# Strassen's scheme for one more state projection, a chunked state tile and more sums by DMA, in a kernel bound by TensorE

## The chip, the cores and the metric

One core of a Trainium2 chip. The metric is device time in microseconds of the whole launch; the profile's span is some 1.8 us shorter than that time, as it runs from the first to the last instruction. The engines are called as the profile has them: PE (TensorE), PEld (its weight loads), DVE (VectorE), ACT (ScalarE), POOL (GpSimd), SP (SyncE).

## The reference

A layer norm feeds two branches: a diagonal complex state-space layer (2048 steps, 512 states) and a gated feed-forward layer (512 to 1792 to 512). Both are added to the input. Cut to what matters:

```python
xn = layernorm(x)                                   # x: 1 x 2048 x 512
Bu = einsum("bld,pd->blp", xn, B_bar)               # state projection (complex)
h  = Lam_bar * h + Bu[:, t]                         # a scan over 2048 steps
y  = 2 * einsum("blp,dp->bld", h, C).real + xn * Dskip
ff = (silu(xn @ w1) * (xn @ w3)) @ w2               # gate, up, down
return x + y + ff
```

## The kernel before

The 2048 tokens go through in four blocks of 512 (blocks 0 to 3). For each block PE computes 14 tiles of gate and up (`glu`), and the state projection `u`. PE writes its results to PSUM tiles; DVE or ACT must take them out before PE can use the tile again. DVE rotates `u` (the `pre` steps), scans it, rotates it back (the `post` steps) and so fills the state slots of the tile `act`, beside the gated products. Then PE multiplies `act` by one joint matrix of `w2` and `C`, in pairs of 128 tokens (pairs 0 to 7, `y_fast`), by Strassen's scheme: seven products for eight, at the price of sums of `act`: s1, s2 and s3 below, and s4 = a12 + s2, made after product 2 of the pair. A filler hands DVE its tasks in an order that it works out from a small model of the two engines. The order is then fixed: each engine runs its own list in order and waits on semaphores.

```python
def post_c(tsl=slice(0, TBLK)):              # last step that fills the states
    a, p16 = act_state(b, hf)[:, :, :, tsl], st["p16"][:, :, :, tsl]
    if (b, hf) == (NBLK - 1, 1):
        nc.vector.tensor_tensor(out=a, in0=a, in1=p16, op=ALU.add)
    else:
        gp.dma_start(out=a, in_=p16, accum_op=ALU.add)     # POOL queue, adds while it moves
...
def row_sums(n, b, p):                       # s3 = a11 - a21, s2 = s3 - a22, s1 = a21 + a22
    ...                                      # a22 holds the second half's states
    return [three, two, one] if n > 5 else [three, one, two]
...
def glu_last(b):                             # block 3: direct tiles first, then groups of four
    ...                                      # up tiles by Strassen: 7 products for 8
    for n in range(NG):
        product(g, a11, b11, True)           # g, e, f, z: four PSUM tiles, used again by each group
        copy(f, g)
        product(e, s1n, t1, True)
        ...
        add(lower[1][:, :, TH:TBLK], g)      # DVE: these adds free g and e for the next group
        product(e, s4n, b22, False)
        add(upper[1][:, :, TH:TBLK], e)
...
last_posts = ssm_tasks(3, middle=[(0.0, after_y2, None), *row_sums(4, *pairs[4])])
```

## Time and profile before

| | |
|---|---|
| time, median of 4 runs | 201.88 us (201.84 to 202.13) |
| span of the profiled run | 200.1 us |
| PE / DVE / ACT busy | 98% / 91% / 67% |
| first tile of block 2 to first tile of block 3 | 86.47 to 140.48: 54.01 us |
| first tile of block 3 to pair 4 | 140.48 to 163.54: 23.06 us |

### The profile page before, as it was taken

What the parts mean: (1) busy time and instruction counts of PE and PEld (TensorE: products, weight loads), DVE (VectorE), ACT (ScalarE), POOL (GpSimd) and SP (SyncE); (2) the same over time, 40 slices, a digit from 0 to 9 for tenths busy, and PEclk for the clock granted to TensorE, in tenths of its full rate; (3) what the DMA queues carried; (4) which work ended last, traced back from release to release, by engine and by line L of the source; (5) the groups of instructions that cost most, each with busy time, mean ns of one, the idle gap of its engine ahead of it and who ended that gap; (6) DMA issues with size and microseconds to landing.
All of it is one profiled execution on the core that took longest, in us unless ns stands there. A gap on an engine that the chain in (4) does not pass through costs nothing.

```text
span 200.1 us, 3642 instructions
## 1 busy us (share of the span) xinstructions
PE 196.5 (98%) x1377; PEld 128.6 (64%) x1377; DVE 181.9 (91%) x255; ACT 133.9 (67%) x277; POOL 49.8 (25%) x71
## 2 busy tenths in 40 slices
PE   8999999999999999999999999999999999999994
PEld 2874444444444488854444468888566668888893
DVE  3699699999999999989999999899999999899862
ACT  3799797699999987967796684362588783111220
POOL 7170279700310132243015013100033103130000
PEclk9999999999999999999999999999999999999999
DMA  6999997990474033944876955560159901994111
GB/s 150 328 276 224 292 168 139 338 268 2 92 147 79 0 65 69 160 131 92 147 140 122 98 101 46 58 135 3 52 105 143 141 2 13 101 142 74 56 41 43
DMA packets 35651, 23.94 MB, mean 120 GB/s; under 512 B 23217, under 2 KB 33585, under 8 KB 35633
## 3 DMA queue, kind: packets, MB, share of 16 engines
q0 software_dynamic: 9520, 10.20, 34.8%
q1 hardware_dynamic: 25536, 13.21, 27.0%
q10 hardware_dynamic: 576, 0.30, 0.7%
q8 instruction: 11, 0.18, 0.4%
q14 instruction: 8, 0.06, 0.1%
HBM read 7.74 MB, written 2.10 MB: 49 GB/s over the span
## 4 chain that ended last, share of the span: by engine, by line
PE 96%; DMA 1%; DVE 1%; SPq 0%; issue 0%; DVEq 0%
PE gu_ps L555 34%; PE gu_ps L982 17%; PE y_ps L982 10%; PE gu_ps L775 7%; PE bu_ps L982 7%; PE y_ps L440 5%; PE bu_ps L440 5%; PE y_ps L797 3%; PE gu_ps L587 2%; PE gu_ps L700 2%; DMA x_blk<-in_A_x_dram 1%; PE bu_ps L797 1%; PE y_ps L700 1%; PE bu_ps L587 1%; PE y_ps L243 1%; PE bu_ps L700 0%
## 5 line engine op out<-in xcount | busy, mean ns | idle before, releaser
L555 PE MATMUL gu_ps<-xnT,w_sb 128*128 128x512 bf16 x312 | 68.2, 379 | 0.0
L555 PEld LDWEIGHTS <-w_sb 128*128 128x128 bf16 x312 | 30.4, 98 | 36.5
L982 PEld LDWEIGHTS <-act 128*128 128x128 f16 x462 | 43.5, 98 | 5.4
L565 ACT ACTIVATE u<-gu_ps 128x512 bf16<-128x512 f32 x41 | 24.8, 605 | 5.8 <-PE gu_ps L555 5.4
L564 ACT ACTIVATE g<-gu_ps 128x512 bf16<-128x512 f32 x41 | 24.7, 603 | 5.1 <-PE gu_ps L555 5.0
L488 DVE TENSOR_TENSOR_SCAN u<-rho,ends,u 128x512 bf16<-128x512 f32 x16 | 19.9, 1270 | 0.0
L507 POOL DMA_DIRECT2D act<-p x7 | 6.4, 908 | 47.1 <-DVE act L498 36.8
L440 PEld LDWEIGHTS <-bt 128*128 128x128 bf16 x96 | 9.4, 98 | 11.3
L982 PE MATMUL gu_ps<-w_sb,act 128*128 128x256 bf16 (+3 forms) x126 | 15.9, 267 | 0.0
L775 PE MATMUL gu_ps<-xnT,w_sb 128*128 128x512 bf16 x64 | 15.9, 379 | 0.0
L573 DVE TENSOR_TENSOR act<-g,u 128x1024 f16<-128x1024 bf16 x21 | 14.2, 678 | 0.0
L787 ACT ACTIVATE g<-gu_ps 128x512 bf16<-128x512 f32 x14 | 8.4, 599 | 5.4 <-PE gu_ps L775 5.0
L936 POOL DMA_DIRECT2D act<-act x4 | 7.7, 1929 | 14.6 <-DVE tw L929 13.7
L440 PE MATMUL bu_ps<-xnT,bt 128*128 128x512 bf16 x48 | 11.3, 379 | 0.0
L440 PE MATMUL y_ps<-xnT,bt 128*128 128x512 bf16 x48 | 11.3, 379 | 0.0
L1005 ACT ACTIVATE x_blk<-gu_ps 128x256 f32<-128x256 f32 (+1 forms) x9 | 3.3, 367 | 10.6 <-PE gu_ps L982 10.6
L982 PE MATMUL bu_ps<-w_sb,act 128*128 128x256 bf16 (+3 forms) x84 | 10.4, 264 | 0.0
L982 PE MATMUL gu_ps<-ct,act 128*128 128x256 f16 (+1 forms) x72 | 10.4, 267 | 0.0
L488 DVE TENSOR_TENSOR_SCAN u<-rho,act,u 128x512 bf16<-128x512 f32 x8 | 10.0, 1271 | 0.0
L494 DVE TENSOR_TENSOR p<-u,tabe 128x2048 f16<-128x2048 bf16 (+1 forms) x9 | 9.9, 1099 | 0.1
L471 DVE TENSOR_TENSOR u<-u,tabe 128x2048 bf16<-128x2048 bf16 x8 | 9.8, 1222 | 0.2
L498 DVE TENSOR_TENSOR act<-u,tabe 128x2048 f16<-128x2048 bf16 (+1 forms) x9 | 9.9, 1097 | 0.0
(189 smaller groups left out, 372.8 us busy)
## 6 DMA issues: line engine op xcount, KB each, us to landing
act<-p POOLq DMA_DIRECT2D x7, 512.0 KB, 4.7
xn<-x_blk POOLq DMA_DIRECT2D x4, 512.0 KB, 5.2
out_dram<-xn SPq DMA_DIRECT2D x15, 128.0 KB, 1.7
w_sb<-in_B_w_dram SPq DMA_DIRECT2D x1, 1792.0 KB, 8.4
w_sb<-in_B_w_dram SPq DMA_DIRECT2D x2, 768.0 KB, 6.3
act<-act POOLq DMA_DIRECT2D x4, 352.0 KB, 7.0
w_sb<-in_B_w_dram SPq DMA_DIRECT2D x4, 256.0 KB, 4.5
w_sb<-in_B_w_dram SPq DMA_DIRECT2D x2, 512.0 KB, 5.9
```

The costliest lines, as they stand in the source:

```text
L440: nc.tensor.matmul(out=ps, lhsT=bt[:, ri, dt, pt * P:(pt + 1) * P], rhs=xnT_blk[b][:, dt, :], start=(dt == 0), stop=(dt == NDT - 1))
L471: nc.vector.tensor_tensor(out=st["g"], in0=st["g"], in1=tabe[:, psl, 0:1, :].to_broadcast(FULL), op=ALU.mult)
L488: nc.vector.tensor_tensor_scan(out=v, data0=rho[:, pt:pt + 1].to_broadcast([P, TBLK]), data1=v, initial=init, op0=ALU.mult, op1=ALU.add)
L494: nc.vector.tensor_tensor(out=st["p16"][:, :, ::-1, tsl], in0=st["g"][:, :, :, tsl], in1=tabe[:, psl, 1:3, tsl], op=ALU.mult)
L498: nc.vector.tensor_tensor(out=act_state(b, hf)[:, :, :, tsl], in0=st["g"][:, :, :, tsl], in1=tabe[:, psl, 0:1, tsl].to_broadcast([P, 2, 2, ...
L555: nc.tensor.matmul(out=ps[:, tsl], lhsT=w[:, dt, f * P:(f + 1) * P], rhs=xnT[:, dt, tsl], start=(dt == 0), stop=(dt == NDT - 1))
L564: nc.scalar.activation(out=g16[:, f % 2, :], in_=g_ps, func=ACT.Silu)
L565: nc.scalar.activation(out=u16[:, f % 2, :], in_=u_ps, func=ACT.Copy)
L573: nc.vector.tensor_tensor(out=act(b)[:, k0:k1 + 1:k1 - k0, :], in0=g16, in1=u16, op=ALU.mult)
L775: nc.tensor.matmul(out=ps, lhsT=w[:, dt, f * P:(f + 1) * P], rhs=xnT[:, dt, :], start=(dt == 0), stop=(dt == NDT - 1))
L787: nc.scalar.activation(out=g16[:, f % 2, :], in_=side(w1_sb, f), func=ACT.Silu)
L982: nc.tensor.matmul(out=out, lhsT=left[:, k, :], rhs=right[k][:, cols], start=(start and k == 0), stop=(k == NK - 1), skip_group_check=True)
```

## The change

Its intent: take an eighth of the columns out of block 2's state projection too, and pay for the sums that this needs by freeing DVE. One set of row sums of the projection matrix serves blocks 2 and 3; it is kept in state slots of block 2's own `act` tile until the states are written there. `act` is laid out by chunks of 128 tokens, so that the sums of pairs move long rows by DMA; four more sums go to DMA; the up scheme does 8 tiles of block 3, not 12. Cut to its core:

```diff
-    NG = 3
+    NG = 2
-    AHEAD = (MID, 8, 4, None)
+    AHEAD = (MID, 8, 1, None)
...
-            act_blk[b] = actp.tile([P, 2 * NK, TBLK], FP16, name="act")
+            act_blk[b] = actp.tile([P, CPB, 2 * NK, P], FP16, name="act")
...
-            def post_c(tsl=slice(0, TBLK)):
-                a, p16 = act_state(b, hf)[:, :, :, tsl], st["p16"][:, :, :, tsl]
+            def post_c(csl=slice(0, CPB)):
+                a, p16 = act_state(b, hf)[:, csl], st["p16"][:, csl]
...
             if f == AHEAD[b]:
-                bu(b)
+                if b == 2:
+                    sin_step(("squares", 3, CPB - 1))
+                    bg.flush(("bu", 0))
+                    steps.extend(bu_fast(b, 0))
+                    second = lambda: bu_fast(b, 1)
+                else:
+                    bu(b)
... (the seven products of each half are then spread over tiles 1 to 5 and 6 to 10)
-        if n in (0, 1, 6, 7):
+        if n in (1, 6, 7):
             one = ... on DVE ...
         else:
             one = (0.0, lambda: gp.dma_start(out=a21, in_=a22, accum_op=ALU.add), ("sums", n))
...
-            if n == 5:
+            if n in (2, 3, 4, 5):
                 gp.dma_start(out=v["s4"], in_=v["s2"], accum_op=ALU.add)
...
-        for i in ((1, 5, 2, 6, 4, 3, 7) if b == 0 else (1, 4, 2, 6, 5, 7, 3)):
+        for i in ((1, 5, 2, 6, 4, 3, 7) if b == 0 else (1, 2, 4, 6, 5, 7, 3) if b == 1 else (1, 4, 2, 6, 5, 7, 3)):
```

More of the change, by code (lines that the diff above doesn't have):

```diff
@@ L420, in act, with act_gates, split, by_state @@
         if act_blk[b] is None:
-            act_blk[b] = actp.tile([P, 2 * NK, TBLK], FP16, name="act")
+            act_blk[b] = actp.tile([P, CPB, 2 * NK, P], FP16, name="act")
         return act_blk[b]
+    def act_gates(b, f):
+        k0, k1 = k_gate(f), k_gate(f + 1)
+        return act(b)[:, :, k0:k1 + 1:k1 - k0, :].rearrange("p c k t -> p k c t")
+    def split(v):
+        return v.rearrange("p k (c t) -> p k c t", t=P)
     def act_state(b, hf):
         k = k_state(2 * hf)
-        return act(b)[:, k:k + 4, :].rearrange("p (j r) t -> p j r t", r=2)
+        return act(b)[:, :, k:k + 4, :]
+    def by_state(v):
+        return v.rearrange("p c (j r) t -> p j r c t", r=2)
     u_blk = {}
@@ L449, in ssm_tasks, with by_chunk @@
         FULL = [P, 2, 2, TBLK]
+        def by_chunk(v):
+            return v.rearrange("p j r (c t) -> p j r c t", t=P)
         def half(hf):
@@ L460, in pre_a @@
                 st["g"] = u_blk[b, hf]
-                if (b, hf) in ((2, 1), (3, 0)):
+                if (b, hf) == (3, 0):
+                    st["p"] = up.tile(FULL, BF16, name="u")
+                elif b > 3:
                     st["p"] = x_blk[b].rearrange("p (j r) t -> p j r t", r=2)
@@ L485, in scan @@
                 elif b > 2:
-                    init = act_blk[b - 1][:, k_state(pt, ri), TBLK - 1:TBLK]
+                    init = act_blk[b - 1][:, CPB - 1, k_state(pt, ri), P - 1:P]
                 v = st["g"][:, j, ri, :]
@@ L489, in scan, with post_a, post_b @@
                                              initial=init, op0=ALU.mult, op1=ALU.add)
-            def post_a(tsl=slice(0, TBLK)):
+            def post_a(csl=slice(0, CPB)):
                 if "p16" not in st:
-                    st["p16"] = ssmw.tile(FULL, BF16, name="p").bitcast(FP16)
-                nc.vector.tensor_tensor(out=st["p16"][:, :, ::-1, tsl], in0=st["g"][:, :, :, tsl],
-                                        in1=tabe[:, psl, 1:3, tsl], op=ALU.mult)
-            def post_b(tsl=slice(0, TBLK)):
-                nc.vector.tensor_tensor(out=act_state(b, hf)[:, :, :, tsl], in0=st["g"][:, :, :, tsl],
-                                        in1=tabe[:, psl, 0:1, tsl].to_broadcast([P, 2, 2, tsl.stop - tsl.start]),
-                                        op=ALU.mult)
-            def post_c(tsl=slice(0, TBLK)):
-                a, p16 = act_state(b, hf)[:, :, :, tsl], st["p16"][:, :, :, tsl]
+                    st["p16"] = ssmw.tile(FULL, BF16, name="p").bitcast(FP16).rearrange(
+                        "p j r (c t) -> p (j r c t)", t=P).rearrange("p (c k t) -> p c k t", c=CPB, t=P)
+                tsl = slice(csl.start * P, csl.stop * P)
+                nc.vector.tensor_tensor(out=by_state(st["p16"][:, csl]), in0=by_chunk(st["g"][:, :, ::-1, tsl]),
+                                        in1=by_chunk(tabe[:, psl, 2:0:-1, tsl]), op=ALU.mult)
+            def post_b(csl=slice(0, CPB)):
+                tsl = slice(csl.start * P, csl.stop * P)
+                n = csl.stop - csl.start
+                nc.vector.tensor_tensor(out=by_state(act_state(b, hf)[:, csl]), in0=by_chunk(st["g"][:, :, :, tsl]),
+                                        in1=by_chunk(tabe[:, psl, 0:1, tsl]).to_broadcast([P, 2, 2, n, P]), op=ALU.mult)
+            def post_c(csl=slice(0, CPB)):
+                a, p16 = act_state(b, hf)[:, csl], st["p16"][:, csl]
                 if (b, hf) == (NBLK - 1, 1):
@@ L520, in add @@
             for fn in fns:
-                bg.add(0.0 if fn in transfers else 1.2, fn, ("scan", b) if fn in scans0 else ("ssm", b))
+                bg.add(0.0 if fn in transfers else 1.2, fn,
+                       ("scan", b) if fn in scans0 else ("post", b) if fn in post0 else ("ssm", b))
         if b == 0:
@@ L528, in ssm_tasks @@
             bg.add(*t)
-        add(*pre1)
+        if b != 2:
+            add(*pre1)
         for t in between:
             bg.add(*t)
+        if b == 2:
+            for t in late:
+                bg.add(*t)
+            add(*pre1)
         add(*scans0)
-        for t in late:
-            bg.add(*t)
+        if b != 2:
+            for t in late:
+                bg.add(*t)
         if posts_last:
@@ L541, in ssm_tasks @@
         add(*post0, *scans1)
-        early, late = ([(0.6, lambda fn=fn, h=h: fn(slice(h * TH, (h + 1) * TH)), ("ssm", b)) for fn in post1]
+        early, late = ([(0.6, lambda fn=fn, h=h: fn(slice(h * CPB // 2, (h + 1) * CPB // 2)), ("ssm", b)) for fn in post1]
                        for h in range(2))
@@ L571, in gate @@
             bg.own(0.6, -0.5)
-            k0, k1 = k_gate(f - 1), k_gate(f)
-            nc.vector.tensor_tensor(out=act(b)[:, k0:k1 + 1:k1 - k0, :], in0=g16, in1=u16, op=ALU.mult)
+            nc.vector.tensor_tensor(out=act_gates(b, f - 1), in0=split(g16), in1=split(u16), op=ALU.mult)
         f0 = 0
+        steps, second = deque(), None
         if b == 0:
@@ L630, in glu @@
                     ssm_tasks(0)
-                bu(b)
+                if b == 2:
+                    sin_step(("squares", 3, CPB - 1))
[4 more added lines that the diff above has]
+                    bu(b)
             g_ps = ps_gu.tile([P, TBLK], FP32, name="gu_ps")
@@ L645, in glu @@
             bg.tensor(1.72)
-            bg.fill((4.0 if f < NFT - 3 else 1.0) if b == 2 else None)
+            if b == 2 and (steps or second):
+                if not steps:
+                    bg.flush(("bu", 1))
+                    bg.flush(("post", b - 1))
+                    steps.extend(second())
+                    second = None
+                for step in steps.popleft():
+                    step()
+                    if len(steps) < 3:
+                        sin_step()
+                    bg.fill(4.0)
+            bg.fill((4.0 if f < NFT - 3 else 2.5) if b == 2 else None)
             if pend and f % 2 == 0:
@@ L659, in run @@
         def run():
-            for fn in column_list(b) + bu_first_sums():
+            for fn in column_list(b):
                 fn()
         run.ready = lambda: ("norm", b, CPB - 1) in sins_done
-        return [(2.1, run, "cols")]
+        return [(1.7, run, "cols")]
     def column_list(b):
@@ L669, in column_list @@
         t1, t2, t3, t4 = (t[:, i] for i in range(4))
-        b11, b12, b21, b22 = (xnT[:, 2 * i:2 * i + 2, j * TH:(j + 1) * TH] for i in range(2) for j in range(2))
+        b11, b12, b21, b22 = quarters(b)
         ups.update(t=(t1, t2, t3, t4), b=(b11, b12, b21, b22))
@@ L677, in bu_quarter, with quarters, spare_slots, bu_rows @@
         return v.bitcast(FP16) if half else v
-    def bu_first_sums():
-        return [lambda hf=hf: nc.vector.tensor_tensor(
-            out=bu_quarter(hf, 0, 1, True), in0=bu_quarter(hf, 0, 1), in1=bu_quarter(hf, 1, 1), op=ALU.add)
-            for hf in range(2)]
+    def quarters(b):
+        return [xnT_blk[b][:, 2 * i:2 * i + 2, j * TH:(j + 1) * TH] for i in range(2) for j in range(2)]
+    def spare_slots(k):
+        return [act(2)[:, i, k:k + 4, :] for i in range(CPB)]
+    def bu_rows(hf):
+        return [v.rearrange("p (r k) t -> p r k t", r=2) for v in spare_slots(k_state(2 * hf))]
@@ new lines, in bu_columns, with bu_sums @@
+    def bu_columns(b):
+        return ups["t"] if b == 3 else [v.rearrange("p (k a) t -> p k (a t)", k=2) for v in spare_slots(k_gate(10))]
+    def bu_sums(b):
+        tasks = []
+        for hf in range(2):
+            a11, a21, a12, a22 = (bu_quarter(hf, *i) for i in ((0, 0), (0, 1), (1, 0), (1, 1)))
+            s1, s2, s3, s4 = bu_rows(hf)
+            tasks.append([(s1, a21, a22, ALU.add), (s2, s1, a11, ALU.subtract), (s3, a11, a21, ALU.subtract),
+                          (s4, a12, s2, ALU.subtract)])
+        t1, t2, t3, t4 = bu_columns(b)
+        b11, b12, b21, b22 = quarters(b)
+        cols = [(*v, ALU.subtract) for v in ((t1, b12, b11), (t2, b22, t1), (t3, b22, b12), (t4, b21, t2))]
+        first = [t for two in zip(tasks[0], cols) for t in two]
+        return [(0.42, lambda out=out, x=x, y=y, op=op: nc.vector.tensor_tensor(out=out, in0=x, in1=y, op=op), ("bu", hf))
+                for hf, part in ((0, first), (1, tasks[1])) for out, x, y, op in part]
@@ L684, in bu_fast @@
     def bu_fast(b, hf):
-        t1, t2, t3, t4 = ups["t"]
-        b11, b12, b21, b22 = ups["b"]
         a11, a12, a22 = bu_quarter(hf, 0, 0), bu_quarter(hf, 1, 0), bu_quarter(hf, 1, 1)
-        s2, s4, s13 = (bu_quarter(hf, *i, True) for i in ((0, 0), (1, 0), (0, 1)))
-        u = up.tile([P, 2, 2, TBLK], BF16, name="u")
+        s1, s2, s3, s4 = bu_rows(hf)
+        t1, t2, t3, t4 = bu_columns(b)
+        b11, b12, b21, b22 = quarters(b)
+        if (b, hf) == (3, 1):
+            u = x_blk[3].rearrange("p (j r) t -> p j r t", r=2)
+        else:
+            u = up.tile([P, 2, 2, TBLK], BF16, name="u")
@@ L690, in bu_fast @@
         s5 = glup.tile([P, 2, TBLK], BF16, name="g16").bitcast(FP32).rearrange("p a t -> p (a t)")
-        if hf == 0:
+        if (b, hf) != (3, 1):
             f, z = (ps_bu.tile([P, TBLK], FP32, name="bu_ps") for _ in range(2))
@@ L708, in parts @@
             return ps.rearrange("p (h t) -> p h t", h=2)
-        def subtract(out, x, y):
-            bg.own(0.4)
-            nc.vector.tensor_tensor(out=out, in0=x, in1=y, op=ALU.subtract)
         def add(out, ps):
@@ L720, in one @@
             copy(f, g)
-            subtract(s2, s13, a11)
         def five():
-            product(e, s13, t1, True)
+            product(e, s1, t1, True)
             copy(s5, e)
-            subtract(s13, a22, s2)
         def two():
             product(f, a12, b21)
-            subtract(s4, a12, s2)
             copy(u[:, 0, :, 0:TH], parts(f))
@@ L737, in seven @@
         def seven():
-            product(g, s13, t3)
+            product(g, s3, t3)
             copy(z, g)
@@ L790, in gate @@
             bg.own(0.6, -0.5)
-            k0, k1 = k_gate(f), k_gate(f + 1)
-            nc.vector.tensor_tensor(out=act(b)[:, k0:k1 + 1:k1 - k0, :], in0=tiles[0], in1=tiles[1], op=ALU.mult)
+            nc.vector.tensor_tensor(out=act_gates(b, f), in0=split(tiles[0]), in1=split(tiles[1]), op=ALU.mult)
         def product(out, left, right, start):
@@ L921, in row_sums @@
         a = act(b)
-        r1, r2 = slice(2 * p * P, (2 * p + 1) * P), slice((2 * p + 1) * P, (2 * p + 2) * P)
-        a11, a12 = a[:, 0:NK, r1], a[:, NK:2 * NK, r1]
-        a21, a22 = a[:, 0:NK, r2], a[:, NK:2 * NK, r2]
+        a11, a12 = a[:, 2 * p, 0:NK, :], a[:, 2 * p, NK:2 * NK, :]
+        a21, a22 = a[:, 2 * p + 1, 0:NK, :], a[:, 2 * p + 1, NK:2 * NK, :]
         s3, s2 = (v.bitcast(FP16).rearrange("p (k t) -> p k t", t=P) for v in homes[n % 2])
@@ L1119 @@
         bg.add(0.7, fn, "tw")
-    bg.add(*difference(0))
+    weight_sum(0, 3)
     first_sums = row_sums(0, *pairs[0])
@@ L1125 @@
         bg.add(1.4, fn, "tw")
+    bg.add(*difference(0))
     bg.add(*first_sums[2])
-    for i, which in ((0, 3), (1, 2), (1, 0), (1, 1), (1, 3)):
+    for i, which in ((1, 2), (1, 0), (1, 1), (1, 3)):
         weight_sum(i, which)
@@ L1141, in keep_ends @@
         kept.add(b)
-        nc.vector.tensor_copy(out=ends, in_=act(b).rearrange("p (h k) t -> p h k t", h=2)[:, :, NFH:NK, TBLK - 1])
+        nc.vector.tensor_copy(out=ends, in_=act(b)[:, CPB - 1].rearrange("p (h k) t -> p h k t", h=2)[:, :, NFH:NK, P - 1])
     ssm_tasks(1, between=[(0.2, lambda: keep_ends(0))])
@@ L1156 @@
     ssm_tasks(2, between=[(0.2, lambda: keep_ends(1)), *row_sums(2, *pairs[2])], late=res_list(3) + column_sums(3))
+    bg.first(bu_sums(2))
     gate = glu(2)
```

## The prediction

> **What bounds the kernel now.** I read the profile page first: busy shares, then the chain of work that ended last.
>
> ```profile
> PE 196.5 (98%) x1377; PEld 128.6 (64%) x1377; DVE 181.9 (91%) x255; ACT 133.9 (67%) x277; POOL 49.8 (25%) x71
> ...
> PE 96%; DMA 1%; DVE 1%; SPq 0%; issue 0%; DVEq 0%
> ```
>
> TensorE (PE) is busy 98% of the 200.1 us span and carries 96% of the chain. But busy can hide pipelined waiting, so I then read the same chain in order of time, to see whether each piece starts where the one before ends.
>
> ```profile
> 59.46 10.36 PE gu_ps L555 x48
> 69.82 1.20 PE y_ps L982 x11
> ...
> 78.22 8.41 PE gu_ps L982 x77
> 86.63 6.92 PE gu_ps L555 x32
> 93.55 1.73 PE bu_ps L440 x8
> 95.28 1.73 PE y_ps L440 x8
> 97.00 1.73 PE bu_ps L440 x8
> 98.73 1.73 PE y_ps L440 x8
> 100.46 17.27 PE gu_ps L555 x80
> 117.72 1.20 PE gu_ps L982 x11
> 118.92 0.87 PE y_ps L700 x8
> ```
>
> Start plus duration gives the next start every time (86.63 + 6.92 = 93.55), from 11.5 us to the last product at 197.4; where the list jumps (146.71 after 144.97 + 0.86) the gap is two 0.44 us pieces too short to be listed. The pace is constant: 10.36/48 = 0.2158 us for a matmul of 512 columns, 8.41/77 = 0.1092 us for one of 256. So there is no stall to win back. Only the number of columns streamed, the 11 us head and the 3 us tail set the time, and the change touches neither head nor tail.
>
> VectorE (DVE) is the engine to fear: 91% over the span, and above 9.5 us in most 10 us stretches. Its timeline shows how little it is ahead in places.
>
> ```profile
> 149.24 1.28 DVE L807 TENSOR_TENSOR u<-y_ps,bt 128x512 bf16<-128x512 f32 x2
> ...
> 180.89 0.88 DVE L929 TENSOR_TENSOR x_blk<-act 128x1408 f16<-128x1408 f16 x1
> 181.81 0.89 DVE L929 TENSOR_TENSOR x_blk<-x_blk,act 128x1408 f16<-128x1408 f16 x1
> ```
>
> The two L807 adds free the PSUM tiles that the next up group overwrites; they end at 150.5, and that group starts at about 150.6 and needs the second tile at about 151.05. The L929 sum ends at 182.7; the product that reads it starts at 179.31 + 3 x 1.20 = 182.9. Slacks of 0.2 to 0.5 us: DVE keeps just ahead and does not hold PE up.
>
> **What the Trainium skill says.** "TensorE: Matmul & The Clock Gate", section "Wait — 56ns, not 53.3ns?": a warm matmul takes its columns over 2.4 GHz plus about 2.5 ns, which is 215.8 and 109.2 ns for 512 and 256 columns. The trace agrees to 0.1 ns, so an eighth fewer columns is nearly an eighth less time, with little lost on twice as many instructions. The same page, "Architectural detail: the array is 16× 32×32, not 1× 128×128", has ACT and DVE as strict FIFOs: one late operand delays everything behind it. "VectorE: DVE Perf Modes", "Mode 2×_1P": two results a cycle need 16-bit data of step 1. The trace agrees: 2048 elements take 1.22 us, and a sum over eleven separate 128-element rows (1408 elements) takes 0.888 us, the same 0.15 us above two per cycle, so cutting rows into chunks of 128 should cost DVE nothing. "DMA: Bandwidth & Descriptors", "Specifications": below 512 B a transfer is read-modify-write and off line rate. The trace agrees:
>
> ```profile
> act<-p POOLq DMA_DIRECT2D x7, 512.0 KB, 4.7
> ...
> act<-act POOLq DMA_DIRECT2D x4, 352.0 KB, 7.0
> ```
>
> The smaller transfer (256 B rows) takes 2.3 us longer than the larger one with 4 KB rows.
>
> **The change, part by part.**
>
> PE, removed: block 2's state projection was 32 matmuls of 512 columns (the four L440 pieces above, 6.92 us). Strassen does it in two halves of seven products of four 256-column matmuls, 56 x 0.1092 = 6.12 us. That is 6.91 - 6.12 = 0.79 us less.
> PE, added: the last block's up projection uses the scheme on 8 tiles, not 12. One group of four tiles goes back from 28 x 0.1092 = 3.06 us to 16 x 0.2158 = 3.45 us: 0.39 us more.
> PE, moved: the block-2 products are spread one step to each gate/up tile 1 to 10 in place of one lump at tile 4, and block 1's output products run 1, 2, 4 in place of 1, 4, 2. No columns in either. Instruction counts of the two builds agree: 24 + 56 - 32 - 12 comes out as +12 matmuls net (56 - 32 = +24, 16 - 28 = -12).
> Net on the path: -0.79 + 0.39 = -0.40 us, 201.86 -> 201.46.
>
> DVE: gone are one s1 sum of pair 0 (0.89) and s4 of pairs 2, 3 and 4 (3 x 0.885 = 2.65), all now accumulating DMAs; a third of three up sums (3 x 0.95 down to about 3 x 0.69, -0.80), one s4 of an up group (0.42) and two PSUM adds (1.37). New are four column sums of block 2 (4 x 0.42 = 1.67) and four PSUM adds (4 x 0.68 = 2.71). The eight row sums for the state projection (8 x 0.42) stay eight, as block 3 reads block 2's set; they only run earlier. Sum: -6.13 + 4.38 = -1.75 us, all beside PE and worth nothing by itself. It pays for the tighter interleaving.
> ACT: 12 copies for 8 in block 2, two fewer in the last block: about +1.2 us on 134, beside PE.
> DMA: four more row-sum accumulates, nine for five, but each moves 2816 B rows in place of 256 B. Estimate, by size from the 4 KB rows: 4 to 4.5 us to landing in place of 7.0. State results go the other way, into 1 KB pieces in place of 4 KB; I take 5 us.
>
> **Rivals.**
>
> (1) A PE stall in the new glu(2). I walked the changed instruction order with durations from the rows. With the pair products ending at 86.6, the eight first sums take 8 x 0.34 from 88.5 and end at 91.2; the product that reads the first two is due at 90.5 (they are there at 89.2), the second pair at 93.1 (there at 89.9). The LN squares of block 3, which the new code forces out first, end at 86.08 in the trace already, so no ACT burst. The overlap of row sums with gate outputs in one tile might make false waits, but the built order shows none on the later products. A slip here would cost 0.2 to 1.5 us.
>
> (2) DVE falls behind because work of block 2 comes later. u of its second half is ready at tile 10, not tile 4, so one rotation and four scans (about 6 us) pass into the output products. Against it stand 2.7 us of row sums already done and 1.8 us of s4 gone from there. My walk has the up sums done at 142.3 and the post-multiply of block 2 at 145.9 (144.9 before), while PE is 0.8 us earlier. The next need is the PSUM adds of the first up group, at 156.1 against PE at 157.2: 1.1 us of slack after 16 us of packed DVE. A chunked state DMA of 6 us in place of 5 would eat most of it, through the s2 sum that waits for it. Then PE waits 0.2 to 0.8 us there.
>
> (3) The DMA s4 is late: issued after product 2, about 120.2, landed about 125.2; product 3 is due at 127.2. The new order gives it four products in place of three. With the old 7.0 us it would stall by some 0.1 us; with contiguous rows I expect no stall.
>
> (4) All is as counted, -0.4 us. As there is no idle PE time to recover, I see no way to gain clearly more.
>
> **Range and chances.** I give the clean case about 70%, and one or two stalls of 0.1 to 0.8 us the rest. The mean of that is a little over 201.46, and I put 201.5. The low end is the clean case less 0.15; the high end takes a stall of 0.7. A 2% change is 4.0 us: ten times what is removed on PE for faster, and for slower a broken overlap on the scale of several DMAs.
>
> **What would show it.** In the chain of the changed kernel, no gap, pieces of 0.44 and 0.87 us between the 1.73 us tiles of block 2, block 2's tiles ending near 116.9 in place of 117.7 (0.8 us earlier), the last up group near 163.3 in place of 163.7, and the last product near 197.0. PE busy down by about 0.4, DVE by 1.7, ACT up by 1.2; act<-act transfers landing in under 5 us. I am wrong if a gap opens in the chain (at 90 to 112: rival 1; at 150 to 160: rival 2; near 127 or 138: rival 3), or if the chunked DVE operations take much over 1.22 us for 2048 elements: doubled, some 14 of them would add over 15 us to DVE and PE would wait.

## The result, and the profile after

The changed kernel took 202.60 us (median of 4 runs, 202.28 to 203.07) against 201.88. The ratio is 1.0035, 95% interval 1.0013 to 1.0057. Here and below a ratio is the mean time of one kernel's runs over that of the kernel before in the same rounds, so it is not quite the ratio of the medians quoted. That is under 2% and so counts as the same, but it is slower, and above the prediction's high end (the clean case of 201.46 and a stall of 0.7).

First where the time came from. The starts of PE's stages in the two traces:

| stage | before | after | difference |
|---|---|---|---|
| start to first full tile of block 0 | 12.67 | 12.80 | +0.13 |
| to first tile of block 2 | 73.80 | 73.79 | -0.01 |
| block 2 and pairs 2, 3, to first tile of block 3 | 54.01 | 53.21 | -0.80 |
| block 3's tiles, to pair 4 | 23.06 | 24.32 | +1.26 |
| pairs 4 to 7, to the last product's end at 197.41 / 197.98 | 33.87 | 33.86 | -0.01 |

Block 2 gave the 0.79 us that were counted. Block 3 should have cost 0.39 us and cost 1.26. The busy line of the page does not show it:

```profile
PE 195.3 (97%) x1376; PEld 129.4 (64%) x1389; DVE 179.6 (89%) x256; ACT 134.5 (67%) x279; POOL 49.9 (25%) x75
```

All 1389 weight loads are there but 13 matmul records are missing, so PE's busy time cannot be used for a difference of half a microsecond. The chain of waits in block 3 can. Its columns are start, duration, and what ran or was waited for:

```profile
145.94 0.56 DVE act L850
146.50 5.95 DMA act<-p
152.45 0.03 issue
...
152.54 0.89 DVE x_blk L986
...
154.37 1.15 DVE xnT L482
...
155.54 1.23 DVE x_blk L486
156.77 0.61 DVE u L865
157.38 0.04 issue
157.43 0.60 PE y_ps L855 x4
158.02 0.60 PE y_ps L855 x4
```

Before, there was PE alone at this place:

```profile
156.30 0.86 PE gu_ps L775 x4
157.16 0.87 PE y_ps L797 x8
```

Now the chain enters by a DMA of 5.95 us: the accumulate that finishes the states of block 2's second half (`post_c`, line 525). DVE's timeline shows who waits; a bracket is idle time before the instruction and what ended it:

```profile
144.73 1.22 DVE L517 TENSOR_TENSOR act<-u,tabe 128x2048 f16<-128x2048 bf16 x1
...
149.80 0.88 DVE L986 TENSOR_TENSOR x_blk<-act 128x1408 f16<-128x1408 f16 x1
152.54 0.89 DVE L986 TENSOR_TENSOR x_blk<-x_blk,act 128x1408 f16<-128x1408 f16 x1 [1.86 <-DMA act<-p]
...
156.69 1.28 DVE L865 TENSOR_TENSOR u<-y_ps,bt 128x512 bf16<-128x512 f32 x2
```

The second L986 is s2 of pair 4, which reads those states. It stands 1.86 us idle, and what is queued behind it comes later, down to the two L865 adds that free the PSUM tiles of the first up group. In the kernel before, the same sum went without a wait:

```profile
151.16 0.88 DVE L929 TENSOR_TENSOR x_blk<-x_blk,act 128x1408 f16<-128x1408 f16 x1
```

PE's own timeline shows the price:

```profile
154.43 0.61 PE L855 MATMUL y_ps<-xnT,w_sb 128*128 128x256 bf16 x4 [0.17 <-DVE w_sb L896]
...
157.43 0.60 PE L855 MATMUL y_ps<-xnT,w_sb 128*128 128x256 bf16 x4 [0.22 <-DVE u L865]
158.02 0.60 PE L855 MATMUL y_ps<-x_blk,bt 128*128 128x256 f16 x4
```

A PE record runs on beyond the start of the next, so the brackets understate. From starts: the product of the first group that reads its s4 (DVE's L896) is due at 153.66 + 4 x 0.1092 = 154.10 and starts at 154.43 (0.33 late); the next group is due at 156.18 + 0.86 = 157.04 and starts at 157.43 (0.39); its second product is due at 157.87 and starts at 158.02 (0.15). Together 0.87 us, which with the counted 0.39 makes the 1.26.

The transfers (KB each, median us from issue to landing):

```profile
act<-p POOLq DMA_DIRECT2D x7, 512.0 KB, 5.8
...
act<-act POOLq DMA_DIRECT2D x5, 352.0 KB, 4.3
```

The chunked layout made the sums of pairs fast (7.0 to 4.3 us) and the state transfers slow (4.7 to 5.8 us). These medians mix transfers that ran alone with transfers that shared their time with others. Here is a state transfer of each kernel that had no other transfer's packets beside it in the trace, before (issued at 145.27) and after (at 105.39):

```profile
act<-p POOLq DMA_DIRECT2D x1, 512.0 KB, 4.6
```

```profile
act<-p POOLq DMA_DIRECT2D x1, 512.0 KB, 5.4
```

So the smaller pieces cost about 0.8 us; a `u<-p` transfer of the same size alone, whose pieces stay at 4 KB, took 4.5 us in both kernels. The transfer that DVE waited for took 5.95: POOL issued its next one at 149.82, and packets of 4 KB ran beside its end. Where the same transfer was issued earlier and had none beside it (e5 and e9 below) it took 5.5. That the rest, some 0.4 us, came from the neighbour fits, but no run tests it alone.

The chunked layout also made them dearer to issue: POOL's instruction for one went from 908 ns to 1316 ns. These are the group rows, of the kernel before and then of the changed one (the two figures ahead of the second bar: busy us, mean ns of one):

```profile
L507 POOL DMA_DIRECT2D act<-p x7 | 6.4, 908 | 47.1 <-DVE act L498 36.8 <-PE gu_ps L982 5.5 <-PE y_ps L982 4.6
```

```profile
L525 POOL DMA_DIRECT2D act<-p x7 | 9.2, 1316 | 36.3 <-DVE act L517 25.2 <-PE gu_ps L834 10.9 <-issue 0.2
```

### The profile page after: what moved, and what is told of

It is laid out like the page before. It is cut to its first block, busy times and chain, and to the rows that moved or that the text cites. A ratio compares the mean times of both kernels' runs of the same rounds, so it can differ in the third digit from the quotient of the medians.

```text
span 200.7 us, 3660 instructions
## 1 busy us (share of the span) xinstructions
PE 195.3 (97%) x1376; PEld 129.4 (64%) x1389; DVE 179.6 (89%) x256; ACT 134.5 (67%) x279; POOL 49.9 (25%) x75
## 4 chain that ended last, share of the span: by engine, by line
PE 86%; DMA 5%; DVE 5%; issue 1%; SPq 1%; DVEq 0%
PE gu_ps L580 33%; PE gu_ps L1039 17%; PE y_ps L1039 10%; PE bu_ps L1039 7%; PE y_ps L450 3%; PE bu_ps L450 3%; PE y_ps L766 3%; DMA act<-p 3%; DMA w_sb<-in_B_w_dram 2%; PE gu_ps L834 2%; PE gu_ps L612 2%; PE gu_ps L766 2%; PE bu_ps L766 1%; PE y_ps L855 1%; PE bu_ps L612 1%
## 5 line engine op out<-in xcount | busy, mean ns | idle before, releaser
L580 PE MATMUL gu_ps<-xnT,w_sb 128*128 128x512 bf16 x304 | 68.9, 379 | 0.4
L580 PEld LDWEIGHTS <-w_sb 128*128 128x128 bf16 x312 | 30.5, 98 | 34.2
L834 PE MATMUL gu_ps<-xnT,w_sb 128*128 128x512 bf16 x77 | 18.4, 379 | 0.2
L525 POOL DMA_DIRECT2D act<-p x7 | 9.2, 1316 | 36.3 <-DVE act L517 25.2
L834 PEld LDWEIGHTS <-w_sb 128*128 128x128 bf16 x80 | 7.8, 98 | 7.5
L450 PEld LDWEIGHTS <-bt 128*128 128x128 bf16 x64 | 6.3, 98 | 7.5
L993 POOL DMA_DIRECT2D act<-act x5 | 4.6, 926 | 21.8 <-DVE tw L986 10.3
L503 DVE TENSOR_TENSOR_SCAN u<-rho,u 128x512 bf16<-128x512 f32 x8 | 9.2, 1207 | 0.0
L1039 PEld LDWEIGHTS <-x_blk 128*128 128x128 f16 x88 | 8.6, 98 | 1.0
L1039 PEld LDWEIGHTS <-tw 128*128 128x128 f16 x88 | 8.6, 98 | 1.0
L486 DVE TENSOR_TENSOR u<-u,tabe 128x2048 bf16<-128x2048 bf16 x7 | 8.6, 1223 | 0.2
L511 DVE TENSOR_TENSOR p<-u,tabe 128x2048 f16<-128x2048 bf16 x7 | 8.5, 1221 | 0.1
```

What stands on the lines that cost most here:

```text
L450: nc.tensor.matmul(out=ps, lhsT=bt[:, ri, dt, pt * P:(pt + 1) * P], rhs=xnT_blk[b][:, dt, :], start=(dt == 0), stop=(dt == NDT - 1))
L486: nc.vector.tensor_tensor(out=st["g"], in0=st["g"], in1=tabe[:, psl, 0:1, :].to_broadcast(FULL), op=ALU.mult)
L503: nc.vector.tensor_tensor_scan(out=v, data0=rho[:, pt:pt + 1].to_broadcast([P, TBLK]), data1=v, initial=init, op0=ALU.mult, op1=ALU.add)
L511: nc.vector.tensor_tensor(out=by_state(st["p16"][:, csl]), in0=by_chunk(st["g"][:, :, ::-1, tsl]), in1=by_chunk(tabe[:, psl, 2:0:-1, tsl]) ...
L580: nc.tensor.matmul(out=ps[:, tsl], lhsT=w[:, dt, f * P:(f + 1) * P], rhs=xnT[:, dt, tsl], start=(dt == 0), stop=(dt == NDT - 1))
L834: nc.tensor.matmul(out=ps, lhsT=w[:, dt, f * P:(f + 1) * P], rhs=xnT[:, dt, :], start=(dt == 0), stop=(dt == NDT - 1))
```

## The experiments

Theory A: the late state DMA stops DVE, which works in order, and PE then waits for what DVE frees. Rival B: DVE has too much work in that stretch, with or without the DMA. Rival C: the loss lies elsewhere (block 2's interleaved products, the chunked layout on DVE, the head). All runs gave correct results and were timed in five rounds, each batch of four on one chip. "Stretch" is from the first tile of block 3 to pair 4 in the trace; without gaps it is 23.05 us for 12 up tiles (the kernel before) and 0.39 more for 8.

| run | time us (range) | ratio to before, 95% interval | stretch us |
|---|---|---|---|
| e0 changed kernel again | 202.25 (202.15-202.40) | 1.0020, 1.0007-1.0033 | 24.22 |
| e1 sums of pair 4 later | 201.42 (200.89-201.74) | 0.9974, 0.9961-0.9987 | 23.44 |
| e2 DMA in two, needed half first | 201.51 (201.32-202.31) | 0.9984, 0.9971-0.9998 | 23.43 |
| e3 DMA in two, needed half last | 203.10 (202.58-203.42) | 1.0054, 1.0041-1.0066 | 24.87 |
| e4 add on DVE, no DMA | 201.90 (201.78-202.05) | 1.0003, 0.9976-1.0030 | 23.74 |
| e5 up sums later | 201.64 (201.34-201.85) | 0.9989, 0.9962-1.0016 | 23.43 |
| e6 up scheme on 12 tiles again | 203.29 (202.72-203.59) | 1.0068, 1.0037-1.0099 | 23.06 |
| e7 before, up scheme on 8 tiles | 202.27 (201.80-202.67) | 1.0021, 0.9992-1.0050 | 23.44 |
| e8 e1, block 2 direct | 203.24 (202.87-204.15) | 1.0065, 1.0042-1.0089 | 23.44 |
| e9 e1 and e5 together | 201.63 (201.26-202.06) | 0.9984, 0.9965-1.0002 | 23.44 |
| e10 e1 again | 201.62 (201.29-201.95) | 0.9981, 0.9964-0.9999 | 23.43 |
| e11 e6, DVE further ahead | 203.64 (203.31-203.88) | 1.0080, 1.0063-1.0098 | 23.05 |

The kernel before took 201.94 us in the batch of e0 to e3, 201.66 (201.27 to 203.22, a wide spread) in that of e4 to e7, and 201.99 in that of e8 to e11. Single launches differ by some 0.3 us in the head, where the first weights and inputs arrive, so the stretch in the trace is the sharper reading for a fraction of a microsecond. The changed kernel itself was run again in the first batch only: from e4 on, what a run gains on it is read from the stretch.

**e0, the changed kernel again.**

> The changed kernel as it is, the control of this batch. Theory A (the accumulating DMA of block 2's second half of states, now in 1 KB pieces, lands after 5.9 us; VectorE, in order, waits for it with everything behind; TensorE then waits for PSUM tiles and s4 in the up groups): 202.3 to 203.0 us, about 0.9 us of TensorE gaps in the last block's up groups, the landing 5.5 to 6.5 us. Rival B (VectorE simply has too much work there, DMA or not): the same here. Rival C (the loss lies elsewhere: block 2's products, chunked layout on VectorE, the head): gaps elsewhere too.

The DVE wait is 1.8 us, the landing 5.9 us, the gaps 0.78 us (24.22 - 23.44). The time of 202.25 us is just under the range expected. The loss repeats in another batch.

**e1, the sums later.** Edit to the changed kernel:

```diff
-    last_posts = ssm_tasks(3, middle=[(0.0, after_y2, None), *row_sums(4, *pairs[4])])
+    last_posts = ssm_tasks(3, middle=[(0.0, after_y2, None)], between=row_sums(4, *pairs[4]))
```

> The row sums of pair 4, the second of which waits for the DMA, are queued behind the second rotation of block 3 (2.4 us of VectorE work), nothing else. A: the VectorE wait for that DMA falls from 1.9 us to under 0.3, the TensorE gaps in the up groups close, 201.45 to 201.7 us. B: the same VectorE work in another order, so the last PSUM adds come as late as before, 202.3 or more. C: 202.3 or more.

```profile
150.78 1.23 DVE L486 TENSOR_TENSOR x_blk<-x_blk,tabe 128x2048 bf16<-128x2048 bf16 x1
...
154.86 1.29 DVE L865 TENSOR_TENSOR u<-y_ps,bt 128x512 bf16<-128x512 f32 x2 [1.12 <-ACT bu_ps L843]
156.07 0.88 DVE L986 TENSOR_TENSOR x_blk<-x_blk,act 128x1408 f16<-128x1408 f16 x1
```

In this DVE timeline the rotation (L486) and the adds (L865) go ahead of s2 (the last line), which no longer waits. The DMA itself still takes 5.9 us. DVE now even waits for the adds' operands, so it was not over-full here. The gap is gone (23.44). The work is the same, the order alone differs, and 0.83 us are back (a little more than expected): A, and against B and C.

**e2 and e3, the DMA in two halves.** They differ in one tuple:

```diff
+                elif (b, hf) == (2, 1):
+                    for i in (0, 2):          # e3: (2, 0)
+                        gp.dma_start(out=a[:, i:i + 2], in_=p16[:, i:i + 2], accum_op=ALU.add)
```

> That one DMA cut in two by chunks, the half that pair 4 needs first; VectorE's work and order are unchanged. A: the first half lands in about 4 us, the wait falls below 0.5 us, the gaps mostly close, 201.5 to 201.9 us. B and C: 202.3 or more.

> The same two half DMAs as in the run before, but the half that pair 4 needs goes second. A: it lands as late as the whole one or later, the wait stays 1.5 to 2.5 us, 202.4 to 203.2 us. B and C: the same as the run before this one, within 0.2 us, as VectorE's work, the bytes and the number of DMAs are equal.

```profile
DVE x_blk L989 <- DMA act<-p: 2.4, 1, 2.4
...
PEld L858 <- DVE w_sb L899: 1.0, 1, 1.0
PE y_ps L858 <- DVE w_sb L899: 0.7, 1, 0.7
```

These are waits of e3 in that stretch (total us, times, longest). In e2 the needed half lands after 3.9 us, and no DVE wait for the DMA is left. With the same bytes, the same two transfers and the same DVE order, the one question of which half goes first is worth 24.87 - 23.43 = 1.44 us in the trace and 1.6 us in the medians. That is the cleanest proof of A: what counts is when the states of chunks 0 and 1 land.

**e4, an add on DVE in place of the DMA.**

```diff
-                if (b, hf) == (NBLK - 1, 1):
+                if (b, hf) in ((2, 1), (NBLK - 1, 1)):
                     nc.vector.tensor_tensor(out=a, in0=a, in1=p16, op=ALU.add)
```

> That DMA replaced by an add on VectorE (128x2048, about 1.2 us more VectorE work just where it is behind). A: 1.2 us of work in place of 1.9 us of waiting, so the gaps shrink to 0.1 to 0.4 us and the time falls to 201.7 to 202.1. B: more VectorE work makes it worse, 202.9 or more. C: about 202.5.

The gaps shrink to 0.30 us (23.74): 1.2 us more work for DVE is better than a wait of 1.86 us. B expected the opposite.

**e5, the up sums later.** The three sums for the up groups go behind block 2's state work, and the flush that forces them moves to the first up group:

```diff
-                    bg.first(up_sums(3))
+                    tasks = list(bg.tasks)
+                    at = 1 + max(i for i, t in enumerate(tasks) if t[2] == ("ssm", 2))
+                    bg.tasks = deque(tasks[:at] + up_sums(3) + tasks[at:])
```

> The three up sums (2 us of VectorE), which with 8 tiles are not needed before the six direct tiles are done, are queued behind the state work of block 2 in place of ahead of it; so the DMA is issued about 2 us earlier. A: it lands before VectorE gets to the sum that needs it, no wait, no gaps, 201.45 to 201.7 us. B: the same VectorE work in the same stretch, 202.3 or more.

The DMA is issued at 144.7 in place of 146.5 us, no wait, no gap (23.43). A second way to the same end.

**e6, 12 up tiles again.** `NG = 2` to `NG = 3`.

> The changed kernel with the up scheme back on 12 tiles, all else kept. By column count this is 0.39 us less TensorE work than the changed kernel and 0.79 less than before. A: the up groups now begin earlier, and the filler puts the row sums of pair 4 about 4 us later in the order, behind the landing of the DMA; a wait under 0.3 us and 201.05 to 201.5 us. B: VectorE has 2.6 us more work in the last block than with 8 tiles, so gaps of over 1 us and 202.3 or more.

A miss. The up groups have no gap (23.06, as in the kernel before), but the time is worse, as PE waits later, at pair 6, for the last DVE add that fills block 3's states (L523):

```profile
PE gu_ps L1039 <- DVE act L523: 1.6, 1, 1.6
```

The time is as B expected, in another variant and another place. PE needed that add at about 180.4 us, and DVE ended it at 182.13, with only 0.9 us of waiting since 167.4; so too much work for DVE is the likely cause, argued from this trace. With 12 up tiles DVE carries about 2.6 us more (an estimate from the rows of the kernel before: 0.8 of up sums, 0.42 of s4, 1.37 of adds), and scans of block 3 slide into pairs 4 and 5.

**e7, the kernel before with 8 up tiles.** `NG = 3` to `NG = 2` there.

> The kernel before with the up scheme on 8 tiles, that one number alone. Column count: one group of four tiles from 28 matmuls of 256 columns to 16 of 512, 0.39 us more, 202.2 to 202.35 us, with no gaps. If the cost of the up groups in the changed kernel came from the 8 tiles themselves (other order of tiles, other fill), this run would have gaps as well and take 202.7 or more.

The stretch is 23.44, 0.38 more than before, with no gap. The 8 tiles cost their columns and nothing else. Here, too, s2 waits for a state DMA (0.8 us), but the slack takes it up.

**e8, e1 with block 2 direct.** `AHEAD` back to tile 4, where `bu(b)` stands in place of the two `bu_fast` halves; both sets of sums are flushed first.

> The kernel of e1 (no gaps) with block 2's state projection direct again, 32 matmuls of 512 columns at tile 4, in place of Strassen's 56 of 256; the row and column sums are still computed. If Strassen's part is worth its column count, this is 0.79 us more than e1: 202.1 to 202.4 us, and the stretch of block 2's tiles 0.8 us longer. If interleaving the products with the tiles cost something that hid part of the gain, it would be 0.3 us more or less than e1.

Half a miss: block 2's own stretch, to pair 2, is 31.08 us against 30.29 in e10, the expected 0.79 more. But the time is 1.6 us above e10's. The rest is a wait for s4 of pair 3, the prediction's third rival. POOL's timeline and PE's wait in e8:

```profile
131.88 1.29 POOL L525 DMA_DIRECT2D act<-p  x1 [8.18 <-PE gu_ps L766]
133.31 0.88 POOL L1078 DMA_DIRECT2D act<-tw  x1
```

```profile
PE bu_ps L1039 <- DMA act<-tw: 0.8, 1, 0.8
```

Now DVE finishes its states earlier, the state DMA is issued just ahead of the s4 sum, and s4 takes 7.4 us to land in place of the 3.9 of the same transfer in e10. There the two are issued the other way round (132.3 and 134.6).

**e9, both mends.**

> Both mends at once (row sums of pair 4 behind the second rotation, up sums behind the state work). Theory A: e1 has no TensorE gap left to close, so this is within 0.2 us of e1, 201.2 to 201.7 us. If some of the time lost were still in that stretch, it would be 0.3 us or more below e1.

Like e10 beside it: with the gap closed there is nothing left for the second mend.

**e10, e1 again.**

> e1 once more, on this chip, as the version to keep: 201.2 to 201.7 us, 0.3 to 0.6 us below the kernel before.

The version to keep. It beats the kernel before in both batches, by 0.3% and 0.2%, and the changed kernel by 0.83 us on the chip where both ran.

**e11, e6 with DVE further ahead in pairs 4 and 5** (`bg.fill()` to `bg.fill(4.0)` there).

> e6 (12 up tiles) missed its expectation: the up groups had no gap, but TensorE waited 1.6 us at pair 6 for the last states. By its trace VectorE has about 13.6 us of work from 167.4 to the add that pair 6 needs at 179.8, so it is over-full by about 1 us, whatever the order, besides 0.9 us of waiting in order. Here the filler lets VectorE run further ahead in pairs 4 and 5, nothing else. If e6 lost to work, a gap of 0.6 to 1.2 us stays (at pair 6 or, as q0 comes later, at pair 4) and the time is 202.2 to 202.9 us; if to order alone, it goes and the time is 201.1 to 201.5 us.

Two waits, of 0.8 us at pair 4 (for q0) and 1.1 us at pair 6:

```profile
PE gu_ps L1039 <- DVE act L523: 1.1, 1, 1.1
PE gu_ps L1039 <- DVE q L1050: 0.8, 1, 0.8
```

Each is in the range expected of one; I expected a single one, and the time is above the range. So the run does not settle work against order. DVE's timeline shows DVE itself idle ahead of the late add, with the last scan and the last state steps of block 3 queued behind a sum that waits for PE:

```profile
178.64 0.42 DVE L1050 TENSOR_TENSOR xn<-gu_ps,q 128x256 bf16<-128x256 f32 x1 [1.60 <-PE gu_ps L1039]
```

In another order those steps might have used the 1.60 us. That DVE is over-full on 12 tiles rests on e6's trace alone and stays open.

## Why the prediction was wrong

- **What bounds the kernel, and the net count of -0.40 us: right.** Block 2's stretch fell by 0.80 us against 0.79 worked out; 8 tiles cost 0.38 to 0.39 us (e7 and all runs without gaps); e1 and e10, which have the change without its gap, come out 0.52 and 0.37 us below the kernel before in medians.
- **DVE, ACT, chunks and the sums' DMAs: right in kind.** DVE's busy time fell by 2.3 us (1.75 worked out), ACT's rose by 0.6 (1.2). Operations on 2048 elements in chunks still take 1.22 us, and the sums' transfers 4.3 us (4 to 4.5). "24 + 56 - 32 - 12" in its count of matmuls is a slip; the bracket behind it is right, and the weight loads rose by its 12 (1377 to 1389).
- **Rivals 1 and 3: right for this kernel.** No gap in block 2's tiles and none for an s4 in pairs 2 and 3. But e8 shows rival 3 to be one reordering away.
- **The step that failed is in rival 2, the term for the state DMA: "I take 5 us".** It measured 5.95 us in the profiled run (5.8 median) and started 0.55 us after the DVE work it follows (0.30 before). 145.9 + 5 puts its landing at 150.9, and DVE came to s2 at 150.68 (149.80 + 0.88), so s2 would hardly have waited; it landed at 152.45, and s2 began at 152.54. The prediction had named the case ("a chunked state DMA of 6 us in place of 5 would eat most of it"), with a PE wait of 0.2 to 0.8 us, and then gave it a share of a 30% chance. A DMA of 5.9 us at this place was the normal case (5.95, and 5.9 in e0, e1 and e10), the slack was used up whole, and PE's wait was 0.87 us, at 154 to 158 us, where the prediction had put the sign of this rival (150 to 160). Its slack of 1.1 us was about right: 1.86 us of DVE's wait less 0.87 of PE's leaves 1.0. But the first need that came late was the s4 of the first up group (0.33 of the 0.87), ahead of the PSUM adds that the walk names. I scaled the sums' transfers by piece size from the trace, but took the state transfers' loss at 0.3 us (4.7 to 5), where it was 1.1 in the medians: some 0.8 for the smaller pieces, and the rest, it seems, where another transfer ran beside.
- **The chances followed from that mistake.** 201.46 + 0.87 + 0.13 (head of the profiled run) = 202.46, against 202.49 for the profiled run. The other runs of that kernel on that chip lie between 202.28 and 203.07. They have no traces, so whether it is the landing or the head that differs among them stays open.

## What to carry to other kernels

A layout that suits one transfer can lengthen another that shares the tile: list every DMA that touches it and size each from a measured one of the same piece length. On an engine that works in order, put a task that waits for a transfer behind the tasks that do not, even if it looks due: here one moved argument turned a loss of 0.2 to 0.35% into a gain of 0.2 to 0.3%. Where the bound engine has no idle time, slack between it and the next engine is what a change spends, so it has to be counted at every hand-over and not on average.

## What the Trainium skill lacked or had wrong

- "DMA: Bandwidth & Descriptors", section "Why small descriptors are slow (HBM only)", says that transfers within SBUF do not suffer. The accumulating ones here do: 352 KB took 7.0 us in pieces of 256 B and 4.3 us in 2816 B; 512 KB took 4.7 us in pieces of 4 KB and 5.8 us in 1 KB (medians; alone 4.6 and 5.4). All are from issue to landing, POOL's own instruction included.
- The same page's "Specifications" puts the line at 512 B. Pieces of 1 KB are above it and still cost about 0.8 us on 512 KB, alone.
- The same page's fit in "Anatomy of one DMA — SWDGE (gpsimd) path", 2.0 us plus bytes over 436 GB/s, gives 3.2 us for 512 KB as an estimate; the accumulates took 4.7 (4 KB pieces) to 5.8 us (1 KB), in medians. The page has no figure for accumulating transfers.
- That section calls descriptor generation "small, variable". POOL's instruction took 0.93 us for 352 KB in pieces of 2816 B, 1.93 us for the same in 256 B, 0.91 us for 512 KB in 4 KB and 1.32 us in 1 KB, in which POOL issues nothing else.
- The pages say that DMAs of one core share the same engines, but none has a figure for two accumulates issued back to back: 352 KB landed after 7.4 us right behind one of 512 KB (e8), after 3.9 us without one ahead of it (e10).
